# Linear attention and two feed-forward layers on one core: a new written-out order for phase one, the backward scan in its own buffer, no floor under the decays

## The chip, the cores and the metric

The kernel runs on 1 core of one Trainium2 chip. The metric is the device time of one execution in microseconds (us). Before the change three timed runs gave a median of 769.39 us (765.54 to 771.35).

## What is computed

```python
def _attn_ref(q, k, v, alpha):                      # B, H, S, D = 4, 8, 768, 48
    for t in range(S):
        state = alpha[:, :, t, :, None] * state + np.einsum('bhd,bhe->bhde', k[:, :, t], v[:, :, t])
        y[:, :, t] = np.einsum('bhd,bhde->bhe', q[:, :, t], state)

def _moe_ref(x, w_in, w_out, g_ln):                 # 3072 tokens, 384 -> 1024 -> 384
    h = x @ w_in
    e = np.exp(h - np.max(h, axis=-1, keepdims=True))
    solu = h * e / (np.sum(e, axis=-1, keepdims=True) + 1e-09)
    mu = np.mean(solu, axis=-1, keepdims=True)
    var = np.mean((solu - mu) ** 2, axis=-1, keepdims=True)
    return ((solu - mu) / np.sqrt(var + 1e-06) * g_ln) @ w_out

def _moe2_ref(x, w_in, w_out):                      # 384 -> 2048 -> 384
    h = x @ w_in
    return (h * np.cos(h)) @ w_out
```

The output of the attention, laid out as 3072 tokens of 384 features, goes through the first layer and then through the second. The weights arrive as 64-bit floats and are turned into 32-bit ones on the chip.

## The kernel before

The 3072 tokens are cut into 24 chunks of 128 tokens (6 chunks to each of 4 batches), numbered 0 to 23. Phase one takes each chunk through the attention and the first layer; phase two takes the second layer in 6 blocks of 512 tokens by 16 slices of 128 hidden units, 96 slots in all.

*Attention of a chunk.* A pack holds queries, keys and decays. `scan_to` (S1, line 256) multiplies the decays up along the chunk; `total_floor` (S2, line 263) writes the four totals, floored at 1e-30, into the start values `d1r` of the backward scan; `total_inverse` (S3, line 266) inverts them; `scan_from` (S4, line 270) scans backward and writes over the decays in the pack. The keys are multiplied by that result (KR on POOL, KV on DVE, line 277), the queries by the forward products (QP on POOL, QV on DVE, line 283). PE then makes the scores `pa` (SC), DVE masks them (MV), PE makes the values `px` (VA), turns the keys (TR) and makes the next state `pst` (ST); DVE adds the state (SD), POOL or ACT decays it (SP, SA).

*First layer of a chunk.* ACT and DVE split the values into a high and a low part (XH, XL), since every product is made of three matmuls in the 32-bit fast format. `hidden` (HD i.0 to i.2, line 392) makes 1024 hidden values in the single tile `ph`. Softmax and norm follow one after another: SM (DVE, maximum), EX (ACT, exponential with its sum), the guard (O1 on DVE, A1 on ACT, line 415), O2 (DVE), O3 (DVE, `so`, line 426), the mean (O4 on DVE, A4 on ACT), SQ (ACT), `variance` PA (ACT, line 444), PW (POOL), PB (ACT), NO (ACT). PE turns the result (TU), ACT and DVE split it (TH, TL), and two chunks together are projected (PR g.f, lines 483 to 490); PX (ACT, line 493) moves the projection to `x2T`. As `ph` and `so` have one buffer each, HD of a chunk waits for O3 of the chunk before.

*Weights.* A weight block is loaded (CL), shifted on DVE (C1, line 186), its sign and low part made on ACT (C2, CA), added on POOL (CD) or DVE (CV), split (WH on ACT, WL on POOL or WV on DVE), and, for the second layer, stored as 32-bit floats (WS). All loads are issued by the SyncE queue (SP), in the order of the list.

*Second layer.* `second_first` (SB, line 721) gives up the attention's memory. w2load (WD) loads a block, w2high (WA, ACT) and w2low (WG, POOL) split it; the loaded block has two buffers. XA (ACT) and XS (DVE) split `x2T`. A slot is h2 (PE), TN (ACT, turns), RS (DVE, residue), CS (ACT, sine of a shifted argument), CM (DVE), SH (ACT), SL (DVE) and three outputs (PE). Slots 0 to 2 are begun inside phase one; the rest come from the function `slot` (line 676), which the change leaves alone. Sine and exponential lie in different tables of ACT, and a load (ACT_TABLE_LOAD) stands where the next one needs the other table.

What sets the order is the written-out list `PLAN` (lines 67 to 118): words such as `S10` or `HD1.0` are called from the first to the last, and every engine gets its instructions in that order. Nothing is moved afterwards; an engine whose next instruction waits lets all those behind it wait.

Of the kernel before, what the change touches and what calls it, by code (L numbers as in the profile page):

```python
# [68 lines left out]
CL7 S21 S31 QP1 TR0 MV0 KT0 CV0 VA0 C21 C11 CA1 S41 ST0 WH0 XH0 LD3 C12 C22 XL0 WL0 CA2 SD0 C23 CV1 CA3 CV2 WH1 KV1
WH2 WV1 C24 TR1 CA4 SC1 S12 KT1 HD0.0 C13 C25 MV1 QP2 CA5 ST1 CV3 VA1 C14 WH3 C15 CV4 C26 CV5 LD4 XH1 WH4 S22 SD1 WL2  # L70
CA6 XL1 SA1 S32 WV3 S42 HD0.1 WH5 WV4 WV5 S13 HD0.2 QV3 S23 S33 KR2 SM0 S43 TR2 EX0 SC2 C16 A10 KT2 CV6 CL8 ST2 O20
KR3 WH6 O30 TR3 O40 C17 HD1.0 C27 MV2 WL6 CA7 SD2 HD1.1 KT3 CL9 CV7 SQ0 HD1.2 C18 SP2 PA0 WH7 ST3 SM1 PW0 VA2 S14 EX1
SC3 S24 LD5 S34 WL7 SD3 PB0 XH2 MV3 NO0 SP3 XL2 A11 TU0.0 C28 O21 TU0.1 C19 CA8 VA3 S44 TH0.0 CL10 O31 CD8 TH0.1 LD6
XH3 XL3 HD2.0 A41 SQ1 S15 HD2.1 C29 QV4 S25 PA1 KV4 WH8 HD2.2 TL0.0 PW1 QP5 TL0.1 SC4 SM2 PB1 NO1 WL8 TR4 MV4 EX2
TU1.0 TU1.1 S35 VA4 S45 KT4 A12 TH1.0 KV5 TH1.1 ST4 O22 O32 XH4 SC5 LD7 CA9 XL4 HD3.0 A42 CD9 SQ2 CL11 MV5 HD3.1 SD4
PA2 PW2 WH9 TL1.0 SP4 HD3.2 TL1.1 S16 PB2 VA5 C210 WV9 NO2 S26 PR0.0 S36 QP6 LD8 SM3 XH5 CA10 S46 EX3 XL5 KR6 TU2.0
A13 PX0.0 TU2.1 O23 TH2.0 PR0.1 O33 TH2.1 TL2.0 A43 SQ3 TL2.1 TR6 S17 PX0.1 SC6 KT6 S27 PA3 S37 QP7 ST6 MV6 PR0.2 PW3
SD6 PB3 NO3 S47 C110 TU3.0 PX0.2 C111 HD4.0 CL12 TH3.0 S18 HD4.1 S28 S38 KR7 TL3.0 HD4.2 QV8 S48 TR7 VA6 KT7 SM4 KR8
SC7 XH6 LD9 EX4 CD10 XL6 ST7 MV7 TR8 TU3.1 SD7 KT8 WS10 SC8 TH3.1 O14 O24 SP7 O34 C211 ST8 VA7 CA11 TL3.1 A44 CL13
CV11 SQ4 HD5.0 MV8 LD10 PA4 XH7 PW4 C212 XL7 HD5.1 WS11 C112 CA12 S19 PR1.0 PB4 CL14 NO4 CV12 QV9 C213 WS12 S29 S39  # L80
CA13 TU4.0 S49 HD5.2 PX1.0 TH4.0 SD8 KR9 VA8 SM5 SP8 TL4.0 EX5 SC9 LD11 C113 CV13 TR9 XH8 CL15 TU4.1 O15 C214 O25 WS13
MV9 PR1.1 CA14 C114 TH4.1 XL8 CD14 CL16 KT9 O35 ST9 PX1.1 VA9 S110 A45 WS14 SQ5 SD9 QP10 HD6.0 PA5 XH9 LD12 TL4.1 C215
PW5 XL9 HD6.1 CA15 SP9 PB5 NO5 S111 HD6.2 C115 TU5.0 S210 CL17 S211 TU5.1 S310 QP11 TH5.0 S311 PR1.2 SM6 TH5.1 CD15
TL5.0 EX6 TL5.1 PR2.0 O16 C216 WS15 O26 O36 PX1.2 CA16 S410 A46 SQ6 HD7.0 KV10 S411 PA6 PX2.0 TR10 SC10 C116 KT10 CV16
CL18 ST10 C117 C217 WS16 HD7.1 SD10 PW6 CA17 KR11 MV10 HD7.2 PB6 CL19 NO6 SP10 SC11 SM7 VA10 S112 EX7 QV12 TU6.0 XH10
LD13 O17 TU6.1 S212 TH6.0 S312 S412 PR2.1 TH6.1 TL6.0 KR12 TL6.1 XL10 PR2.2 PX2.1 O27 O37 C118 A47 SQ7 CV17 HD8.0 S113
WS17 PX2.2 PA7 C218 TR12 S213 S313 PW7 HD8.1 MV11 KT12 PB7 NO7 S413 HD8.2 CA18 C119 TU7.0 SM8 KR13 CL20 TU7.1 TH7.0
ST12 TH7.1 TL7.0 CD18 VA11 EX8 TL7.1 TR13 O18 C219 LD14 SD12 PR3.0 CA19 O28 O38 WS18 XH11 CL21 KT13 O48 QV13 SQ8 HD9.0
XL11 CV19 PX3.0 PA8 HD9.1 C220 WS19 PW8 S114 CA20 HD9.2 PB8 NO8 S214 C120 PR3.1 QV14 CL22 SM9 CD20 S314 EX9 C121 WS20
PR3.2 S414 PX3.1 C221 O19 KV14 CA21 O29 CV21 CL23 TR14 PX3.2 TU8.0 KT14 C122 WS21 TU8.1 TH8.0 ST13 O39 TH8.1 SC12 C222  # L90
TL8.0 HD10.0 A49 SQ9 TL8.1 MV12 HD10.1 PA9 CA22 PW9 SD13 PB9 CL24 HD10.2 NO9 C123 CV22 VA12 SM10 SP13 C223 WS22 SC13
CA23 LD15 XH12 CD23 TU9.0 MV13 EX10 CL25 TU9.1 ST14 XL12 TH9.0 SC14 WS23 C124 A110 C224 O210 O310 VA13 TH9.1 CA24
TL9.0 HD11.0 SD14 LD16 XH13 CD24 A410 SQ10 XL13 HD11.1 MV14 SP14 PA10 WS24 C225 TL9.1 HD11.2 PW10 CA25 S115 PB10 VA14
NO10 S215 SM11 QP15 TU10.0 XH14 LD17 S315 PR4.0 S116 EX11 XL14 QP16 TH10.0 TL10.0 PR4.1 S216 O111 PX4.0 C125 CV25 O211
WS25 S415 TU10.1 PX4.1 S316 KR15 PR4.2 O311 TH10.1 TL10.1 S416 HD12.0 PX4.2 O411 KR16 SQ11 HD12.1 PA11 PW11 HD12.2
PB11 NO11 TR15 SM12 TR16 KT15 TU11.0 KT16 TU11.1 SC15 TH11.0 TH11.1 TL11.0 ST15 EX12 TL11.1 ST16 SD15 PR5.0 O112 O212
SP15 O312 S117 A412 SQ12 PR5.1 S217 S317 QV17 PA12 PX5.0 S417 MV15 PW12 HD13.0 PX5.1 KR17 PB12 NO12 VA15 SC16 SD16
XH15 LD18 HD13.1 XL15 SP16 MV16 HD13.2 SC17 SM13 VA16 EX13 S118 TU12.0 A113 S218 XH16 LD19 O213 QP18 S318 TU12.1 MV17
TH12.0 PR5.2 TH12.1 O313 S418 HD14.0 PX5.2 O413 TL12.0 KR18 SQ13 HD14.1 TL12.1 S119 PA13 HD14.2 S219 S319 PW13 XL16
PB13 TR18 S419 NO13 VA17 QV19 KT18 SM14 KR19 ST18 XH17 LD20 SC18 XL17 EX14 SD18 TR19 A114 MV18 TU13.0 KT19 TU13.1  # L100
TH13.0 ST19 O214 O314 TH13.1 SC19 TL13.0 A414 VA18 SQ14 SD19 HD15.0 LD21 MV19 XH18 SA19 XL18 HD15.1 TL13.1 PA14 PW14
HD15.2 S120 PB14 NO14 S220 PR6.0 S320 QP20 SM15 S420 EX15 KV20 TU14.0 PX6.0 TU14.1 O115 TH14.0 O215 S121 TR20 TH14.1
# [5 lines left out]
XL22 HD18.1 HD18.2 VA23 SM18 EX18 TU17.0 TU17.1 PR7.1 TH17.0 O118 O218 O318 TH17.1 XH23 TL17.0 A418 SQ18 TL17.1 HD19.0
XL23 PA18 PX7.1 PW18 SB WD0 XA0 HD19.1 WD1 PB18 WD2 XS0 NO18 WD3 HD19.2 XA1 XA2 XS1 TU18.0 WA0 TU18.1 XS2 PR7.2 SM19
WG0 WA1 EX19 WG1 H20 A119 PX7.2 O219 O319 WA2 WA3 WG2 HD20.0 A419 TN0 SQ19 HD20.1 RS0 PA19 TH18.0 HD20.2 PW19 CS0  # L110
TL18.0 WG3 PB19 CM0 H21 TH18.1 SM20 NO19 TL18.1 EX20 PR8.0 A120 TN1 O220 SH0 RS1 TU19.0 PX8.0 TU19.1 TH19.0 SL0 PR8.1
TH19.1 O320 CS1 CM1 O420 SH1 TL19.0 HD21.0 SQ20 TL19.1 SL1 HD21.1 PA20 PX8.1 PW20 PB20 HD21.2 NO20 PR8.2 SM21 EX21
TU20.0 A121 PX8.2 O221 TU20.1 TH20.0 PR9.0 O321 TH20.1 TL20.0 O421 TL20.1 SQ21 HD22.0 PA21 PX9.0 PW21 HD22.1 PB21 NO21
HD22.2 TU21.0 SM22 TU21.1 TH21.0 PR9.1 TH21.1 TL21.0 EX22 TL21.1 O122 O222 O322 PR9.2 PX9.1 A422 SQ22 HD23.0 PA22
PX9.2 PW22 PB22 NO22 HD23.1 HD23.2 TU22.0 SM23 TU22.1 TH22.0 PR10.0 TH22.1 TL22.0 EX23 TL22.1 O123 O223 O323 PR10.1
PX10.0 A423 SQ23 PR10.2 PA23 PX10.1 PW23 PB23 NO23 TU23.0 PX10.2 TU23.1 TH23.0 H22 TH23.1 TL23.0 TL23.1 PR11.0 TN2 RS2
PR11.1 PX11.0 PR11.2 PX11.1 PX11.2
# [828 lines left out]
```

## Time and profile before

| | us |
|---|---|
| median of three timed runs | 769.39 |
| the profiled execution's own time | 772.82 |
| its span, first to last instruction | 771.0 |
| busy: PE / DVE / ACT / POOL | 734.4 / 598.5 / 443.9 / 148.6 |
| chain that ended last, share of PE / DVE / ACT | 67% / 9% / 6% |

PE's matmuls overlap in the profile, so its busy time shows where it stood idle, and not how fast it went; the granted clock (PEclk, 1.00 is 2.4 GHz and 0.50 is 1.2 GHz) is read beside it. An arrow in square brackets names what ended an engine's idle time before the instruction.

### The profile page before, as it was taken

Reading aid. Unit: us, or ns where it says so; the run is one execution under the profiler, and the core shown is the slowest. Engines: PE = TensorE matmul, PEld = TensorE weight load, DVE = VectorE, ACT = ScalarE, POOL = GpSimd, SP = SyncE. Lnnn points to the kernel's source line nnn. Section 1 sums busy time; section 2 is a strip of 40 time slices with the busy share of each in tenths; the row PEclk is TensorE's granted clock in tenths of the full one; section 3 lists DMA queues with packets and bytes.
Section 4 is the critical chain, followed back from the end, with each engine's and each line's share of the span. In section 5 each row is a group of like instructions: output and inputs, shape, how many; then the busy total and the mean of one; then the engine's idle time right before and its main releaser. Section 6 shows DMA issues by size and latency. Waiting matters only on the chain.

```text
span 771.0 us, 13377 instructions
## 1 busy us (share of the span) xinstructions
PE 734.4 (95%) x5260; PEld 612.5 (79%) x5260; DVE 598.5 (78%) x997; ACT 443.9 (58%) x748; POOL 148.6 (19%) x139
## 2 busy tenths in 40 slices
...
GB/s 237 260 134 153 114 231 256 163 282 264 34 87 87 88 43 62 21 1 1 84 88 102 62 102 103 34 144 76 82 62 110 82 83 140 85 101 92 14 1 45
DMA packets 27959, 81.15 MB, mean 105 GB/s; under 512 B 3600, under 2 KB 6928, under 8 KB 27888
## 3 DMA queue, kind: packets, MB, share of 16 engines
...
q14 instruction: 28, 0.23, 0.1%
...
## 4 chain that ended last, share of the span: by engine, by line
PE 67%; DVE 9%; ACT 6%; DMA 3%; issue 2%; POOL 1%; ACTq 0%; DVEq 0%; POOLq 0%
PE o L625 7%; PE ph L400 7%; PE o L623 7%; PE h L576 7%; PE o L624 7%; PE h L578 7%; PE h L577 7%; PE po L488 4%; PE po L489 3%; PE po L490 3%; PE px L333 2%; PE pl L467 2%; DVE wup L653 2%; PE pa L302 2%; DVE r L590 1%
## 5 line engine op out<-in xcount | busy, mean ns | idle before, releaser
L596 ACT ACTIVATE g<-r,halfpi 128x512 f32<-128x512 f32 x96 | 69.6, 725 | 117.8 <-DVE r L590 117.8
L625 PE MATMUL o<-gl,w2h 128*128 128x512 f32 x288 | 114.2, 397 | 2.3 <-DVE gl L611 2.3
L623 PE MATMUL o<-gh,w2h 128*128 128x512 f32 x288 | 113.4, 394 | 0.0
L576 PE MATMUL h<-x2h,w2h 128*128 128x512 f32 x288 | 113.4, 394 | 0.0
L577 PE MATMUL h<-x2l,w2h 128*128 128x512 f32 x288 | 113.2, 393 | 0.0
L624 PE MATMUL o<-gh,w2l 128*128 128x512 f32 x288 | 113.2, 393 | 0.0
L578 PE MATMUL h<-x2h,w2l 128*128 128x512 f32 x288 | 113.1, 393 | 0.0
L583 ACT ACTIVATE n<-h,quarter 128x512 int32<-128x512 f32 x96 | 65.9, 686 | 72.5 <-PE h L578 72.2
L589 DVE SCALAR_TENSOR_TENSOR r<-n,h 128x512 f32<-128x512 int32 x96 | 65.9, 686 | 48.8 <-ACT n L583 48.5
L601 DVE TENSOR_TENSOR g<-g,h 128x512 f32<-128x512 f32 x96 | 66.1, 688 | 34.2 <-ACT g L596 34.2
L488 PE MATMUL po<-lth,wout_h 128*128 128x256 f32 x288 | 83.3, 289 | 2.8 <-ACT x2T L494 2.8
L489 PE MATMUL po<-ltl,wout_h 128*128 128x256 f32 x288 | 81.5, 283 | 0.0
L490 PE MATMUL po<-lth,wout_l 128*128 128x256 f32 x288 | 81.4, 283 | 0.0
L590 DVE SCALAR_TENSOR_TENSOR r<-n,r 128x512 f32<-128x512 int32 x96 | 70.3, 732 | 3.3
L625 PEld LDWEIGHTS o<-gl,w2h 128*128 128x128 f32 x288 | 54.1, 188 | 17.4 <-DVE gl L611 5.1
L611 DVE TENSOR_TENSOR gl<-g,gh 128x512 fp32r<-128x512 f32 x96 | 66.1, 688 | 0.8 <-ACT gh L606 0.8
L624 PEld LDWEIGHTS o<-gh,w2l 128*128 128x128 f32 x288 | 54.2, 188 | 12.5
L577 PEld LDWEIGHTS h<-x2l,w2h 128*128 128x128 f32 x288 | 54.2, 188 | 12.4
L578 PEld LDWEIGHTS h<-x2h,w2l 128*128 128x128 f32 x288 | 54.1, 188 | 12.3
L576 PEld LDWEIGHTS h<-x2h,w2h 128*128 128x128 f32 x288 | 54.1, 188 | 12.3
L623 PEld LDWEIGHTS o<-gh,w2h 128*128 128x128 f32 x288 | 54.1, 188 | 11.9
L606 ACT ACTIVATE gh<-g 128x512 fp32r<-128x512 f32 x96 | 59.8, 623 | 2.8 <-DVE g L601 2.3
(117 smaller groups left out, 1432.6 us busy)
## 6 DMA issues: line engine op xcount, KB each, us to landing
...
wraw<-w SPq DMA_DIRECT2D x32, 384.0 KB, 3.1
...
w2f<-top SPq DMA_DIRECT2D x16, 384.0 KB, 5.8
w2r<-w2f SPq DMA_DIRECT2D x16, 384.0 KB, 2.9
...
```

The lines of the kernel that those rows point to most:

```text
L488: PE.matmul(po, wout_h[:, k, fs], lh[:, k, :], start=k == 0, stop=False)
L489: PE.matmul(po, wout_h[:, k, fs], ll[:, k, :], start=False, stop=False)
L490: PE.matmul(po, wout_l[:, k, fs], lh[:, k, :], start=False, stop=k == NF1 - 1)
L576: PE.matmul(ph, wh[:, ks], xh[:, k, :], start=k == 0, stop=False)
L577: PE.matmul(ph, wh[:, ks], xl[:, k, :], start=False, stop=False)
L578: PE.matmul(ph, wl[:, ks], xh[:, k, :], start=False, stop=k == KT - 1)
L590: V.scalar_tensor_tensor(out=r, in0=n, scalar=-C2, in1=r, op0=ALU.mult, op1=ALU.add)
L596: A.activation(g, r, AF.Sin, bias=halfpi)
L601: V.tensor_tensor(Gs[b, c], Gs[b, c], ph, ALU.mult)
L623: PE.matmul(po, wh[:, fs], gh, start=c == 0, stop=False)
L624: PE.matmul(po, wl[:, fs], gh, start=False, stop=False)
L625: PE.matmul(po, wh[:, fs], gl, start=False, stop=c == NF2 - 1)
```

## The change

The list is replaced by another (1123 words instead of 1147). In it no CS stands ahead of EX23, the last exponential; S2 is gone; the first loads, the last chunks of attention and the start of the second layer stand elsewhere. KV appears 13 times instead of 9 and KR 11 instead of 15, QP 14 instead of 12 and QV 10 instead of 12, CD 13 instead of 9 and CV 13 instead of 17, A1 17 instead of 11 and O1 7 instead of 13, SA 8 instead of 4 and SP 8 instead of 12. S4 writes into a buffer R of its own (two of them); d1r has one buffer instead of two; S3 reads the forward products directly; the padding rows of the first packs hold ones where they held zeros. A1 and PA are copies with a constant added, where they were Identity with a bias tile. The table of range checks (`out`) moves into a pool of phase two.

```diff
 PLAN = """
-LP0 LP1 MK LQ0 CL0 LQ1 LV0 ID S10 CL1 CL2 S20 CL3 S30 S40 CL4 CL5 LP2 KV0 LQ2 QV0 GL C20 LV1 C10 SC0 CA0 LV2 S11 CL6
...
+LP0 LP1 LP2 GL MK LQ0 LQ1 CL0 S10 CL1 CL2 S11 CL3 ID LV0 S30 S40 LQ2 LV1 LV2 QV0 KV0 QV1 SC0 S31 C20 C10 S41 CA0 C21
...
-        T["out"] = fl.tile([128, NCHK + NWB], F32, name="out")
...
-        tiny = cst.tile([128, 1], F32, name="tiny")
-        guards = cst.tile([128, 1], F32, name="guards")
...
-        d1r = [at.tile([128, AW], F32, name=f"d1r{j}", bufs=1) for j in range(2)]
+        d1r = at.tile([128, AW], F32, name="d1r", bufs=1)
...
-        def total_floor(i):
-            V.tensor_scalar(d1r[i % 2][:, C + 1::C + 1], T["P", i][:, :, C], 1e-30, None, ALU.max)
...
         def total_inverse(i):
-            total = d1r[i % 2][:, C + 1::C + 1]
-            V.reciprocal(total, total)
+            V.reciprocal(d1r[:, C + 1::C + 1], T["P", i][:, :, C])
...
         def scan_from(i):
...
-            V.tensor_tensor_scan(out=dec[:, back], data0=dec[:, back], data1=d1r[i % 2][:, back], initial=0.0,
+            R = at.tile([128, AW], F32, name=f"R{i}", tag="R", bufs=NR)
+            V.tensor_tensor_scan(out=R[:, back], data0=dec[:, back], data1=d1r[:, back], initial=0.0,
                                  op0=ALU.mult, op1=ALU.add)
+            T["R", i] = pairs(R[:, 1:])[:, :, 1:C + 1]
...
         def keys(i, eng=G):
...
-            K, R = pairs(pk[:, NP * C:2 * NP * C]), pairs(pk[:, 2 * NP * C + 1:])[:, :, 1:C + 1]
+            K, R = pairs(pk[:, NP * C:2 * NP * C]), T["R", i]
...
             else:
-                A.activation(c[:, 1:2], c[:, 1:2], AF.Identity, bias=guards)
+                A.activation(c[:, 1:2], c[:, 1:2], AF.Copy, bias=1e-9)
...
         def variance(i):
             c = T["c", i]
-            A.activation(c[:, 5:6], c[:, 4:5], AF.Identity, scale=1.0 / FF1, bias=tiny)
+            A.activation(c[:, 5:6], c[:, 4:5], AF.Copy, scale=1.0 / FF1, bias=1e-6)
...
-        for t in d1r + states:
+        for t in [d1r] + states:
...
-        G.memset(tiny, 1e-6)
-        G.memset(guards, 1e-9)
...
+            T["out"] = pools["q3"].tile([128, NCHK + NWB], F32, name="out", bufs=1)
...
-                   GL=lambda: SP.dma_start(gln, a["gln"]), S1=scan_to, S2=total_floor, S3=total_inverse, S4=scan_from,
+                   GL=lambda: SP.dma_start(gln, a["gln"]), S1=scan_to, S3=total_inverse, S4=scan_from,
...
+    pack0[..., 2 * NP * C:PW - 1] = np.arange(AW - 1) % (C + 1) > 0
```

DVE at the start of the program (P are the forward products, R the result of the backward scan, pk the packs, mage the first shifted weights), before:

```order
L259 SCALAR_TENSOR_TENSOR P_157<-pk_123,d1p 128x516
L264 TENSOR_SCALAR d1r_121<-P_157 128x4
L268 RECIPROCAL d1r_121<-d1r_121 128x4
L272 SCALAR_TENSOR_TENSOR pk_123<-pk_123,d1r_121 128x516
L280 TENSOR_TENSOR pk_123<-pk_123 128x512
L285 TENSOR_TENSOR pk_123<-pk_123,P_157 128x512
L186 TENSOR_SCALAR mage<-rawi_151 128x512
L259 SCALAR_TENSOR_TENSOR P_193<-pk_124,d1p 128x516
L264 TENSOR_SCALAR d1r_122<-P_193 128x4
L268 RECIPROCAL d1r_122<-d1r_122 128x4
```

and in the changed kernel (line numbers are its own, 4 or 5 less):

```order
L256 SCALAR_TENSOR_TENSOR P_149<-pk_119,d1p 128x516
L256 SCALAR_TENSOR_TENSOR P_155<-pk_120,d1p 128x516
L262 RECIPROCAL d1r<-P_149 128x4
L267 SCALAR_TENSOR_TENSOR R_163<-pk_119,d1r 128x516
L281 TENSOR_TENSOR pk_119<-pk_119,P_149 128x512
L276 TENSOR_TENSOR pk_119<-pk_119,R_163 128x512
L281 TENSOR_TENSOR pk_120<-pk_120,P_155 128x512
L262 RECIPROCAL d1r<-P_155 128x4
L183 TENSOR_SCALAR mage<-rawi_147 128x512
L267 SCALAR_TENSOR_TENSOR R_185<-pk_120,d1r 128x516
```

Two forward scans now come first, S2 is no longer there, the product of the queries stands ahead of that of the keys, and the second chunk's queries follow at once.

The SyncE queue at the start, which issues the loads (rawi are blocks of the first weights, pk packs, v values), before:

```order
L240 DMA pk_123<-pack 128x1024
L180 DMA rawi_151<-win 128x1024
L240 DMA pk_124<-pack 128x1024
L247 DMA v_154<-vpack 128x448
L727 DMA ident<-ident 128x128
L180 DMA rawi_159<-win 128x1024
L180 DMA rawi_161<-win 128x1024
L180 DMA rawi_164<-win 128x1024
L180 DMA rawi_168<-win 128x1024
L180 DMA rawi_170<-win 128x1024
```

and in the changed kernel (line numbers are its own, 4 or 5 less):

```order
L237 DMA pk_120<-pack 128x1024
L177 DMA rawi_147<-win 128x1024
L177 DMA rawi_151<-win 128x1024
L177 DMA rawi_153<-win 128x1024
L177 DMA rawi_157<-win 128x1024
L722 DMA ident<-ident 128x128
L244 DMA v_160<-vpack 128x448
L237 DMA pk_121<-pack 128x1024
L244 DMA v_166<-vpack 128x448
L244 DMA v_168<-vpack 128x448
L177 DMA rawi_194<-win 128x1024
L177 DMA rawi_218<-win 128x1024
```

The third pack's decays are loaded third of all (above these rows); its queries and keys and two more blocks of values now stand ahead of the fifth and sixth weight blocks.

ACT where the last chunks of phase one meet the first slots (e is the exponential, g the sine, w2h the high part of a weight block of the second layer, x2h that of its input, n the turns), before:

```order
L438 ACTIVATE c_3636<-c_3636 128x1
L583 ACTIVATE n_0_3669<-h_0_0_3643,quarter 128x512
L442 ACTIVATE e_3640,c_3636<-so_3656,c_3636 128x1024
L446 ACTIVATE c_3636<-c_3636,tiny 128x1
L475 ACTIVATE lth_3682<-pl_0_3599 128x4x128
L596 ACT_TABLE_LOAD
L596 ACTIVATE g_0_3692<-r_0_3678,halfpi 128x512
L454 ACTIVATE c_3636<-c_3636 128x1
L475 ACTIVATE lth_3682<-pl_1_3605 128x4x128
L459 ACTIVATE so_3656<-so_3656,c_3636 128x1024
L412 ACT_TABLE_LOAD
L412 ACTIVATE e_3713,c_3709<-ph_3661,c_3709 128x1024
```

and in the changed kernel (line numbers are its own, 4 or 5 less):

```order
L548 ACTIVATE w2h_3813<-w2r_3811 128x768
L548 ACTIVATE w2h_3817<-w2r_3815 128x768
L548 ACTIVATE w2h_3824<-w2r_3822 128x768
L490 ACTIVATE x2T<-po_1_3897 128x256
L434 ACTIVATE c_3876<-c_3876 128x1
L438 ACTIVATE e_3881,c_3876<-so_3922,c_3876 128x1024
L442 ACTIVATE c_3876<-c_3876 128x1
L559 ACTIVATE x2h_3834<-x2T 128x512
L450 ACTIVATE c_3876<-c_3876 128x1
L408 ACTIVATE e_3987,c_3982<-ph_3931,c_3982 128x1024
L455 ACTIVATE so_3922<-so_3922,c_3876 128x1024
L490 ACTIVATE x2T<-po_2_3957 128x256
```

Before, the sine of slot 0 stands ahead of an exponential with a table load on either side; now three blocks of w2 are split in a row, then a chunk's square, the last part of x2h and the last exponential follow, and no table load is among them.

## Rows read from the trace of the kernel before

**Rows 1.** Windows: from:to, length, PE, PEld, DVE, ACT, POOL busy, PEclk, DMA share, GB/s.

```profile
0.00:20.00 20.00, 11.62 (x78) 6.37 (x78) 15.20 (x24) 9.49 (x15) 5.07 (x15) 0.91 0.66 230
20.00:40.00 20.00, 14.55 (x128) 10.70 (x130) 17.32 (x24) 8.98 (x17) 4.48 (x3) 0.76 0.85 249
40.00:60.00 20.00, 13.70 (x196) 10.82 (x192) 18.40 (x25) 15.22 (x27) 10.06 (x7) 0.91 0.61 166
...
180.00:200.00 20.00, 17.75 (x224) 16.05 (x223) 16.04 (x28) 11.88 (x23) 7.37 (x7) 1.00 0.77 209
...
300.00:320.00 20.00, 17.16 (x91) 15.28 (x90) 10.93 (x19) 17.09 (x28) 4.22 (x3) 0.83 0.22 70
```

**Rows 2.** Timeline of PE, 40 to 62 us: start us, us, engine, line, op, tiles [idle before <-releaser].

```profile
44.15 1.19 PE L400 MATMUL ph<-win_h,xh 128*128 128x512 f32 x2 [1.53 <-DVE so L429]
...
60.76 1.22 PE L400 MATMUL ph<-win_h,xh 128*128 128x512 f32 x2 [2.66 <-DVE so L429]
```

**Rows 3.** Groups by line of DVE, only 0 to 60.2 us.

```profile
L264 DVE TENSOR_SCALAR d1r<-P 128x4 f32<-128x4 f32 x5 | 1.9, 370 | 0.2
```

**Rows 4.** Timeline of DVE, 0 to 30 us.

```profile
4.97 0.17 DVE L264 TENSOR_SCALAR d1r<-P 128x4 f32<-128x4 f32 x1
...
7.99 0.69 DVE L280 TENSOR_TENSOR pk<-pk 128x512 f32<-128x512 f32 x1 [1.37 <-DMA pk<-pack]
...
10.87 1.18 DVE L264 TENSOR_SCALAR d1r<-P 128x4 f32<-128x4 f32 x1
...
23.12 1.23 DVE L259 TENSOR_TENSOR_SCAN P<-pk,d1p 128x516 f32<-128x516 f32 x1 [2.54 <-DMA pk<-pack]
```

**Rows 5.** Timeline of POOL, 0 to 30 us.

```profile
10.84 1.18 POOL L285 TENSOR_TENSOR pk<-pk,P 128x512 f32<-128x512 f32 x1 [8.23 <-DVE P L259]
```

**Rows 6.** Groups by line, whole run: count | busy us, mean ns | idle before us.

```profile
L557 POOL TENSOR_TENSOR w2l<-w2r,w2h 128x768 fp32r<-128x768 f32 x16 | 29.6, 1853 | 37.1 <-ACT w2h L553 37.1
...
L367 DVE TENSOR_TENSOR S<-pst,S 64x256 f32<-64x256 f32 x32 | 13.3, 417 | 2.0 <-PE px L333 1.5 <-PE pst L351 0.2
...
L442 ACT ACTIVATE e<-so,c 128x1024 f32<-128x1024 f32 x24 | 27.6, 1151 | 3.9 <-DVE c L436 2.1 <-DVE d1r L264 1.1
...
L564 ACT ACTIVATE x2h<-x2T 128x512 fp32r<-128x512 f32 x18 | 11.0, 616 | 0.0
...
L186 DVE TENSOR_SCALAR top<-raw 128x768 int32<-128x768 int32 x16 | 11.0, 691 | 1.0 <-DMA w2f<-top 1.0
...
L446 ACT ACTIVATE c<-c,tiny 128x1 f32<-128x1 f32 x24 | 7.0, 292 | 0.6
...
L264 DVE TENSOR_SCALAR d1r<-P 128x4 f32<-128x4 f32 x24 | 6.9, 292 | 0.6
...
L438 ACT ACTIVATE c<-c 128x1 f32<-128x1 f32 x15 | 3.0, 201 | 8.6 <-DVE so L429 8.6
...
L412 ACT ACT_TABLE_LOAD x2 | 2.6, 1283 | 0.0
```

**Rows 7.** Timeline of ACT, 296 to 324 us.

```profile
305.69 0.58 ACT L475 ACTIVATE lth<-pl 128x512 fp32r<-128x512 f32 x1
...
306.29 1.28 ACT L596 ACT_TABLE_LOAD   x1
```

**Rows 8.** Timeline of PE, 305 to 321 us.

```profile
307.77 0.28 PE L490 MATMUL po<-lth,wout_l 128*128 128x256 f32 x1
...
310.22 0.28 PE L490 MATMUL po<-lth,wout_l 128*128 128x256 f32 x1
...
314.37 0.58 PE L488 MATMUL po<-lth,wout_h 128*128 128x256 f32 x1 [2.84 <-ACT x2T L494]
...
314.96 0.41 PE L490 MATMUL po<-lth,wout_l 128*128 128x256 f32 x1
...
319.44 0.41 PE L490 MATMUL po<-lth,wout_l 128*128 128x256 f32 x1
```

**Rows 9.** DMA issues by line: count, KB each, median us to landing.

```profile
w2r<-w2f SPq DMA_DIRECT2D x16, 384.0 KB, 2.9
```

More of the change, by code (lines that the diff above doesn't have):

```diff
@@ L39 @@
 NPK = 3
+NR = 2
 LA = 4
@@ L67 @@
 PLAN = """
-LP0 LP1 MK LQ0 CL0 LQ1 LV0 ID S10 CL1 CL2 S20 CL3 S30 S40 CL4 CL5 LP2 KV0 LQ2 QV0 GL C20 LV1 C10 SC0 CA0 LV2 S11 CL6
[L69 to L102, printed above, removed]
```

63 lines of the change are left out of this document (48 added, 15 removed).

## The prediction

> **What bounds the kernel now.** I read the windows first, by stage [rows 1]. In the first 60 us PE is busy for 11.6, 14.6 and 13.7 of 20 us each, while DVE is busy for 15.2, 17.3 and 18.4: DVE leads there. From 80 us on PE shows idle time only here and there (2.25 us in 180 to 200), and in 300 to 320, where the first slots of phase two meet the last exponentials: 2.84 us idle and a granted clock of 0.83. So the rest of the kernel is PE's own work, which the change leaves as it is, and what can be won or lost lies at those two places.
>
> Then I asked what ends PE's waits in the start. Both times that PE waits for the hidden matmuls of the next chunk (44.15 and 60.76 us) it is DVE's `so` (L429, word O3) that lets it go [rows 2]. DVE's queue up to O30 and O31 therefore sets when chunks 1 and 2 begin.
>
> **The start.** Up to O31 the old and the new list give DVE almost the same work. Out go five S2, which took 1.9 us together [rows 3]; behind O31 move one shift, C19 (0.69 by its group's mean), and the two instructions of SD3 (2 x 0.42) [rows 6]. Two key and query products leave this stretch and two others enter it, with the same shape and cost. Sum: 1.9 + 0.7 + 0.8 = 3.4 us less.
>
> DVE also waits less for loads, or for others. Before, the forward scan at 23.12 us waited 2.54 us for the third pack [rows 4]; LP2 now stands third of all loads, so this wait goes. The 1.37 us wait for the queries and keys [rows 4] stays in its place, though 0.26 MB more lies ahead of them, since a second forward scan of 1.23 us stands in the gap. What is late next is the fifth weight block: LQ2, LV1 and LV2 (0.52 + 2 x 0.23 = 0.98 MB by their shapes in the order) now stand in front of it, and at the 230 to 249 GB/s of these windows [rows 1] that is up to 4.1 us; it is nothing if the block's buffer comes free later than that anyway. What queues behind its shift C14 on DVE is XL0, and for that PE waits with the first hidden matmuls. I take 1.0 us, nearer to nothing, because DVE has its scans, masks and adds of four blocks in front of C14. Start: 3.4 + 2.5 - 1.0 = 4.9 us earlier.
>
> At one place a rule bears on this. The S2 at 4.97 us took 0.17 us; the one at 10.87 took 1.18, and began and ended with POOL's product at 10.84 [rows 4, 5]: DVE stood still while POOL ran. The Trainium skill (SBUF — State Buffer, Who interferes with whom) says that the two share a port pair, that whoever comes first holds it for its whole instruction, and that this holds for two-port modes of DVE and for DVE instructions with two SBUF inputs. By that rule the new list can lose as well as win, since CD puts four more adds on POOL: it is the slower rival below, where its price comes from rows.
>
> **The stretch from 60 to 300 us.** The other 19 S2 cost 6.9 - 1.9 = 5.0 us of DVE [rows 3, 6], beside a PE that has work. Its idle time here that rows name is the 2.25 us [rows 1]; the rest is nothing or small. Bounds 0 and 2.3 us, or a loss of as much where the new order waits elsewhere; I take 1.0 us. The copies in place of Identity (PA 24 times, A1) save 0.29 - 0.20 = 0.09 us each [rows 6], on ACT, and A1 takes six guards from DVE: nothing, since PE's other chunk covers the chain, and at most some tenths where it doesn't. Writing R instead of the pack costs DVE nothing (same shape, 1.2 us); two buffers make S4 of chunk i wait for the keys of chunk i - 2, long done. d1r with one buffer is written and read by DVE alone, in order. Four more SA fall on ACT, which is idle for two fifths of the span; if ACT were bound they would cost 4 x 4 x 0.3, some 5 us, at the 0.29 us of PA's row [rows 6].
>
> **The junction.** Before, ACT loads the sine's table at 306.29 us and the exponential's again after it, 1.28 us each [rows 6, 7], twice over ahead of the last exponential. PE waits 2.84 us for an `x2T` copy that is behind them at ACT, and then goes at half clock: three projection matmuls take (319.44 - 314.96) / 7 = 0.64 us instead of (310.22 - 307.77) / 7 = 0.35 [rows 8], over eight such triplets 2.3 us. Together 5.1 us. Of five loads (three of the sine, two of the exponential) one is left, and it stands after the last exponential, beside three projections.
>
> What is late next: ACT now splits the w2 blocks 1, 2 and 3 in a row. Block 3 needs block 1 split by POOL (1.85) and its load (2.9) [rows 6, 9], so 4.75 us after WA1, and ACT has only WA2 in between. Queued behind are PX, A4, SQ22 (1.15 and its accumulator read), PA and XA2 (0.62) [rows 6], then XS2 on DVE, and H20 on PE waits for it: some 4.75 + 0.85 + 2.75 + 0.7 = 9.05 us after WA1, which ends some 0.5 us after PE begins HD23. PE has HD23 and PR9.2 before H20: 18 matmuls of 512 columns and 24 of 256 at the full pace [rows 8], 4.2 + 2.8 = 7.0 us. So PE waits about 2.5 us. Bounds: 0, if the earlier blocks leave ACT free sooner, and 4.75 with another spell at half clock. Junction: 5.1 - 2.5 = 2.6 us.
>
> A rule would make this larger. The load at 306.29 starts as the copy before it ends (305.69 + 0.58) [rows 7], so each costs ACT its 1.28 us and no more. The Trainium skill (ScalarE: Activation LUTs, What ACT_TABLE_LOAD costs) gives 2.66 us to each switch, with a drain of 1.38; by that the four loads that go would be worth up to 5.5 us more. The trace does not agree.
>
> **Sum.** 4.9 + 1.0 + 2.6 = 8.5 us. The profiled execution took 772.8 us (span 771.0 and 1.8 around it), so 764.3; it lies 3.4 above the median of the timed runs, and against that median, 769.4, I predict 760.9 us. One per cent, 7.7 us, is about what a measurement of this kernel can tell from no change.
>
> **Rivals.**
> - *The start gains nothing*: the fifth block comes the full 4.1 us late, or DVE's shorter queue ends in another wait. For it: PE's waits in the start end with DVE after loads [rows 2, 4]. Against it: five S2 are gone in any case. Gain 3.6, so 765.8 us.
> - *POOL blocks DVE (slower)*. POOL is busy for 5.1 + 4.5 + 10.1 = 19.6 us of the first 60 [rows 1]. If about half of that already holds DVE up, as S2 at 10.87 suggests for its share, a list that lets all of it do so loses 10 us more: -8.5 + 10 gives 770.9 us. It decides from 8.5 us of added blocking on. Against it: KR's four moves take work from POOL.
> - *The clock falls at the junction again*: the 2.5 us wait and 2.3 us at half clock, as before. Gain 6.2, so 763.2 us.
> - *More is won*: no wait at the junction and no late block: 4.9 + 1.0 + 1.0 + 5.1 = 12.0, so 757.4 us.
>
> **How the numbers follow.** Forecast 0.50 (its own range 756 to 766), start gains nothing 0.20, POOL blocks 0.10, clock 0.12, more 0.08. Faster by over 1% means under 761.7: a little over half of the forecast, all of the last rival, and a part of the clock's (0.28 + 0.08 + 0.09): 0.45. Slower by over 1% needs POOL's rival and lost time later too: 0.07. Within 1%: 0.48. The range, 753 to 771, reaches from below the last rival to the slower one.
>
> **What would show it.** In the changed kernel's trace: hidden matmuls of chunk 2 begin near 56 us instead of 60.8; no S2; one sine load, and none of the exponential's after the first; a PE wait of 2 to 3 us ahead of slot 0's first matmul, and PEclk near 1.00 there. The prediction is wrong if chunk 2 begins no earlier, if DVE's two-input instructions stretch beside POOL more than now, or if PE finds new waits between 60 and 300 us.

## The result, and the profile after

| | before | after |
|---|---|---|
| median us | 768.89 (4 runs, 765.54 to 771.35) | 756.35 (4 runs, 755.58 to 756.80) |
| ratio, 95% interval | | 0.9839 (0.9813 to 0.9866) |
| profiled execution, its span | 772.82, 771.0 | 756.13, 754.2 |
| busy PE / DVE / ACT / POOL | 734.4 / 598.5 / 443.9 / 148.6 | 730.0 / 582.7 / 438.8 / 154.4 |

The gain is 12.5 us between the medians, where 8.5 was forecast; the two profiled executions lie 16.7 apart, because that of before was a long one. Besides being shorter, the runs after lie within 1.2 us of each other, those of before within 5.8.

The same windows as [rows 1], of the changed kernel (length, then busy us of PE, PEld, DVE, ACT, POOL, then PEclk, DMA share and GB/s):

```profile
0.00:20.00 20.00, 13.00 (x82) 7.79 (x82) 14.07 (x21) 9.52 (x16) 6.72 (x13) 0.83 0.92 338
20.00:40.00 20.00, 15.11 (x200) 11.02 (x201) 19.05 (x31) 14.40 (x27) 7.36 (x5) 0.83 0.75 186
40.00:60.00 20.00, 18.50 (x240) 15.16 (x240) 18.63 (x28) 19.09 (x36) 11.40 (x9) 1.00 0.71 189
180.00:200.00 20.00, 20.00 (x273) 17.98 (x272) 15.05 (x25) 10.80 (x22) 4.61 (x4) 1.00 0.29 61
300.00:320.00 20.00, 20.00 (x179) 18.05 (x178) 9.69 (x16) 12.46 (x24) 6.42 (x4) 1.00 0.16 46
```

PE has 4.8 us more work in 40 to 60 us, no idle time in the two later windows, and full clock in 300 to 320 us, where it had 0.83. In 60 to 300 us its idle time falls from 4.1 to 1.9 us.

PE's timeline where [rows 2] showed it waiting for chunks 1 and 2 (start us, us, operation, idle time before):

```profile
39.62 0.70 PE L396 MATMUL ph<-win_h,xh 128*128 128x512 f32 x2 [1.46 <-DVE so L425]
...
50.37 0.73 PE L396 MATMUL ph<-win_h,xh 128*128 128x512 f32 x2
```

Chunk 1's hidden matmuls start 4.5 us earlier, and chunk 2's 10.4 us earlier and without a wait.

DVE's timeline in the start, the places that answer to [rows 4] and the two instructions that were longest for their kind:

```profile
3.58 2.36 DVE L256 TENSOR_TENSOR_SCAN P<-pk,d1p 128x516 f32<-128x516 f32 x2 [2.05 <-DMA pk<-pack]
...
9.44 0.69 DVE L281 TENSOR_TENSOR pk<-pk,P 128x512 f32<-128x512 f32 x1 [0.77 <-DMA pk<-pack]
...
16.51 1.41 DVE L198 CUSTOM_DVE_ANT_0 magso<-magso,rawi 128x1024 uint16<-128x1024 uint16 x1 [0.28 <-ACT rawi L194]
...
25.19 1.23 DVE L256 TENSOR_TENSOR_SCAN P<-pk,d1p 128x516 f32<-128x516 f32 x1
...
26.78 0.17 DVE L262 RECIPROCAL d1r<-P 128x4 f32<-128x4 f32 x1
...
35.98 2.11 DVE L267 TENSOR_TENSOR_SCAN R<-pk,d1r 128x516 f32<-128x516 f32 x1
...
48.36 1.28 DVE L425 SCALAR_TENSOR_TENSOR so<-e,c,ph 128x1024 f32<-128x1024 f32 x1
```

Two forward scans in a row start at 3.58; the queries and keys cost a wait of 0.77 where it was 1.37; the scan of the third pack, which had waited 2.54, waits for nothing at 25.19. `so` of chunk 1 starts at 48.36 where it started at 59.45.

So the start won 11.1 us on DVE, and the forecast accounts for less than half of it. The rest shows in the trace of before once DVE and POOL are read side by side. DVE before, instructions that took longer than others of their line:

```profile
15.38 1.43 DVE L186 TENSOR_SCALAR mage<-rawi 128x512 int32<-128x512 int32 x1
...
26.44 1.41 DVE L186 TENSOR_SCALAR mage<-rawi 128x512 int32<-128x512 int32 x1
...
34.22 1.67 DVE L221 TENSOR_TENSOR win_l<-magso,win_h 128x512 fp32r<-128x512 f32 x1
...
51.12 2.20 DVE L259 TENSOR_TENSOR_SCAN P<-pk,d1p 128x516 f32<-128x516 f32 x1
...
56.67 2.86 DVE L272 TENSOR_TENSOR_SCAN pk<-pk,d1r 128x516 f32<-128x516 f32 x1
```

and POOL before, in the same stretch:

```profile
14.73 1.81 POOL L221 TENSOR_TENSOR win_l<-mage,win_h 128x512 fp32r<-128x512 f32 x1 [2.70 <-ACT win_h L215]
26.05 1.51 POOL L285 TENSOR_TENSOR pk<-pk,P 128x512 f32<-128x512 f32 x1 [9.52 <-DVE am L318]
...
33.80 1.54 POOL L280 TENSOR_TENSOR pk<-pk 128x512 f32<-128x512 f32 x1 [4.80 <-DVE pk L272]
...
50.40 1.83 POOL L221 TENSOR_TENSOR wout_l<-topo,wout_h 128x768 fp32r<-128x768 f32 x1 [1.27 <-ACT wout_h L215]
...
56.33 2.10 POOL L201 TENSOR_TENSOR topo<-topo,lowo 128x768 int32<-128x768 int32 x1 [0.91 <-ACT lowo L197]
```

Each of the five starts while a POOL instruction runs, and ends 0.3 to 1.1 us after it: the shift at 15.38 lies beside POOL's 14.73 to 16.54 and takes 1.43 in place of 0.42. Three more (27.77, 40.79 and 47.46 us) and S2 at 10.87 [rows 4, 5] did the same. Against what the same instructions take elsewhere (0.17, 0.42, 0.55, 0.67, 0.95, 1.23), the nine lose 9.2 us. In the changed kernel only the add at 16.51 (1.41 for 0.69) and the scan at 35.98 (2.11 for 1.23) do: 1.6 us. POOL isn't less busy there (25.5 us in the first 60, where it was 19.6): it runs beside other DVE instructions. From the first scan to that `so` DVE is busy for 40.2 of 44.8 us, where it was 49.8 of 55.8: its waits fell by 1.4 us only, and of the 9.6 us less of busy time 7.6 are POOL's and some 2.0 are work.

The junction in the changed kernel, ACT's timeline at its last split of a w2 block, the last part of `x2h` and the first sine:

```profile
319.45 0.85 ACT L548 ACTIVATE w2h<-w2r 128x768 fp32r<-128x768 f32 x1 [4.03 <-DMA w2r<-w2f]
...
322.07 0.62 ACT L559 ACTIVATE x2h<-x2T 128x512 fp32r<-128x512 f32 x1
...
327.27 1.28 ACT L591 ACT_TABLE_LOAD   x1
```

PE's timeline there, at chunk 23's first hidden matmul, slot 0's first and the turns behind it:

```profile
315.92 0.63 PE L396 MATMUL ph<-win_h,xh 128*128 128x512 f32 x2
...
322.92 0.39 PE L571 MATMUL h<-x2h,w2h 128*128 128x512 f32 x1
...
325.47 1.09 PE L463 MATMUL pl<-ident,so 128*128 128x128 f32 x8 [0.33 <-ACT so L455]
```

ACT waits 4.03 us for w2 block 3, much as forecast, and PE doesn't wait: slot 0 starts at 322.92, right behind its predecessor, and the next wait, for the norm, is 0.33. Only one table load for the sine is left (327.27), and behind it none for the exponential.

### The profile page after: what moved, and what is told of

Its sections match the earlier page's. It is cut to its first block, busy times and chain, and to the rows that moved or that the text cites. A ratio compares the mean times of both kernels' runs of the same rounds, so it can differ in the third digit from the quotient of the medians.

```text
span 754.2 us, 13336 instructions
## 1 busy us (share of the span) xinstructions
PE 730.0 (97%) x5260; PEld 606.5 (80%) x5260; DVE 582.7 (77%) x965; ACT 438.8 (58%) x766; POOL 154.4 (20%) x134
## 4 chain that ended last, share of the span: by engine, by line
PE 44%; DVE 8%; ACT 3%; issue 1%; ACTq 0%
PE o L620 7%; PE h L571 7%; PE h L573 7%; PE h L572 7%; PE o L618 7%; PE o L619 7%; DVE wup L648 2%; DVE r L584 2%; DVE r L585 2%; ACT g L591 1%; DVE g L596 1%; DVE wup L649 1%; PE po L484 1%; PE po L485 1%; PE po L486 1%
## 5 line engine op out<-in xcount | busy, mean ns | idle before, releaser
L618 PEld LDWEIGHTS o<-gh,w2h 128*128 128x128 f32 x288 | 54.1, 188 | 12.6 <-ACT x2T L490 0.2
```

Source lines behind the costliest of these rows:

```text
L618: PE.matmul(po, wh[:, fs], gh, start=c == 0, stop=False)
```

## The experiments

Two theories. **W** (work and loads, the record's own): the start is won by less DVE work and by the third pack's load. **P** (POOL): the new list puts POOL's work beside DVE instructions that it doesn't hold up. For the end of phase one, **J**: the order of sine and exponential is what cost there. Medians, each with its ratio to runs of the kernel before on the same chip. Differences below are between the medians; "by the ratios" means that each version is first set against before on its own chip:

| run | us (runs) | ratio, 95% interval |
|---|---|---|
| changed kernel | 756.35 (4) | 0.9839 (0.9813 to 0.9866) |
| old_order | 765.44 (10) | 0.9968 (0.9948 to 0.9988) |
| new_start | 763.43 (10) | 0.9938 (0.9914 to 0.9963) |
| new_late | 767.82 (10) | 0.9997 (0.9975 to 1.002) |
| new_to_3 | 760.43 (6) | 0.9899 (0.9865 to 0.9934) |
| old_to_14 | 764.18 (10) | 0.9944 (0.9916 to 0.9972) |
| pool_small | 763.31 (10) | 0.9932 (0.9903 to 0.9961) |
| pool_busy | 763.66 (10) | 0.9938 (0.9918 to 0.9958) |
| late_pack | 755.46 (4) | 0.9833 (0.9792 to 0.9875) |
| floor_back | 758.85 (6) | 0.9883 (0.9859 to 0.9907) |
| sine_early | 760.61 (6) | 0.9913 (0.9888 to 0.9938) |
| keep_warm | 755.93 (6) | 0.9852 (0.9827 to 0.9877) |
| both | 756.05 (6) | 0.983 (0.9793 to 0.9866) |

### Which stretch carries the gain

Five kernels have the changed code and a list put together from the two. In the first three, chunk 10's backward scan starts from chunk 11's totals (the old list has S3 of 11 ahead of S4 of 10, and `d1r` has one buffer now).

**old_order** (against the changed kernel, as all diffs here but one)

```diff
 PLAN = """
-LP0 LP1 LP2 GL MK LQ0 LQ1 CL0 S10 CL1 CL2 S11 ...
+LP0 LP1 MK LQ0 CL0 LQ1 LV0 ID S10 CL1 CL2 CL3 ...
```

> The changed code with the old list, its 24 S2 words struck out. Theory W (work and loads: the start is won by less DVE work and the earlier third pack, the junction by the table loads): only the floors go, 1.9 us in the start and about 1 later, so hidden matmuls of chunk 2 near 59 us (60.8 before) and about 766 us. Theory P (POOL: the new list is faster at the start because DVE stands still beside POOL for some 1.6 us there and not for 9): the list carries the gain, and the 1.0 us that S2 stood still at 10.87 us passes to the next DVE instruction, so chunk 2 at 59.5 us or later and 767 to 769 us.

2.5 us faster than before by the ratio (1 to 4). The time is W's (P had 767 to 769), and chunk 2's hidden matmuls come at 56.4 us, earlier than either theory had it. In DVE's timeline, the mask at the place where S2 had stood still, and the scan of the third pack:

```profile
10.93 1.21 DVE L314 TENSOR_TENSOR am<-pa,mask 128x1024 f32<-128x1024 f32 x1
...
21.31 1.23 DVE L256 TENSOR_TENSOR_SCAN P<-pk,d1p 128x516 f32<-128x516 f32 x1 [2.49 <-DMA pk<-pack]
```

The 1.0 us of S2 didn't pass on, as P had it: the reciprocal and the mask that stand there now take 0.18 and 1.21. Up to `so` of chunk 1 DVE stands still beside POOL for 5.0 us, in six instructions, where it was 9.2 in nine: part of that went with the code alone. The wait for the third pack stays. The code carries about a fifth of the gain, the order the rest.

**new_start** and **new_late**: up to HD4.0 the new list, then the old; and up to HD18.0 the old, then the new.

> The changed code; the new list up to HD4.0, from there the old one without S2. Both theories W and P: the start's gain is kept, hidden matmuls of chunk 4 near 80 us (91.2 before) and 758 to 761 us, with the two sine loads and PE's 2.8 us wait near slot 0 still there. Rival K (the time won at the start is only lent, and the old order waits for it later): chunk 4 near 80 us but over 765 us.

> The changed code; the old list without S2 up to HD18.0, then the new one. Junction theory J (the sine's and the exponential's table loads and the half clock behind PE's wait cost about 5 us): one sine load, no wait of PE over 1 us and a granted clock of 1.00 between chunk 20 and slot 2, and 763 to 765 us. Rival: the junction is gained only because phase one arrives there with DVE and ACT ahead, by the start: under 2 us less than the old list with the new code.

Neither came in at its forecast time: new_start is 2.0 us under old_order, new_late 2.4 over it, and both for the way they were cut. In new_start chunk 4 begins at 79.3 us, as expected; then PE waits, since the words that the old list has for it there were done in the new prefix. In new_late HD19 to HD21 stand without the scores, values and projections that the whole new list puts between them. PE in new_start:

```profile
83.29 0.66 PE L463 MATMUL pl<-ident,so 128*128 128x128 f32 x4 [2.31 <-ACT so L455]
```

and in new_late, one of three such waits:

```profile
285.54 0.73 PE L396 MATMUL ph<-win_h,xh 128*128 128x512 f32 x2 [1.38 <-DVE so L425]
```

A list may only be cut where both have done the same words, so the cuts were made again there.

**new_to_3**: new up to LD7 (the load of chunk 7's pack and values), just ahead of chunk 3 (four words differ), then old. **old_to_14**: old up to NO13 (one word differs), then new.

> The changed code; the new list up to LD7, just before chunk 3's hidden matmuls, where both lists have done the same words but four; from there the old list (S3 of chunk 11 one word later). Theory P or W, the start's gain is the start's own: chunk 3 at 60.5 to 61 us as in the changed kernel (66.9 with the old list and the new code), kept through chunk 5 this time, and 759 to 761.5 us against 765.4 of the old list with the new code. Rival K (lent only): chunk 3 at 61 but chunk 12 again near 191 us, as with the old list, and 763 us or more.

> The changed code; the old list up to NO13, where both lists have done the same words but one, then the new list, with one table load for the sine. Theory J (table loads and the half clock behind the wait): no wait of PE over 0.6 us between 280 and 340 us, granted clock 1.00 there, 4 to 5 us less than the old list with the new code: 760.5 to 761.5 us. Rival (the junction is gained only with a start that is ahead): 763.5 us or more, with waits of PE for `so` between chunks 18 and 22.

new_to_3 gains 0.69% more than old_order by the ratios, 5.3 us: the start. Chunk 3 begins at 59.1 us, 7.8 us ahead of old_order, and 3.6 of these are gone by chunk 12 (187.4 against 191.6 us), so rival K holds in part. PE's timeline in new_to_3:

```profile
176.47 0.65 PE L463 MATMUL pl<-ident,so 128*128 128x128 f32 x4 [1.97 <-ACT so L455]
```

and ACT's:

```profile
173.01 1.10 ACT L190 ACTIVATE low<-raw 128x768 bf16<-128x768 f32 x1 [2.10 <-DMA raw<-w]
```

ACT waits for the load of a w2 block, then PE for ACT: the old list has its weights too late for a program that is ahead. This wait, and some 1.6 us at the lower clock behind it (0.57 granted in 177 to 181 us), are most of the 3.6. The changed kernel has no wait of PE in 165 to 190 us; its list stands one to two weight blocks further at chunk 8.

old_to_14 has PE idle for 0.38 us in 300 to 340 us, at full clock, and without a wait between chunks 18 and 22, as J has it, but its time is the rival's: 0.24%, 1.8 us under old_order by the ratios (1.3 in the medians, 3.6 in the profiled executions, 762.43 and 766.04). The runs of both spread over 4 to 5 us. The traces say more: from the norm of chunk 13 (NO13) to slot 0's first output old_to_14 takes 130.6 us and old_order 134.0, so the new end is worth 3.3 us there, in one execution of each.

### POOL beside DVE

**pool_small** (the kernel before; the low parts are set to zero beforehand)

```diff
-            eng.tensor_tensor(lo, w, hi.bitcast(F32), ALU.subtract)
+            m = 32 if eng is G and n in (0, 2, 6, 7) else w.shape[1]
+            eng.tensor_tensor(lo[:, :m], w[:, :m], hi.bitcast(F32)[:, :m], ALU.subtract)
...
-            eng.tensor_tensor(K, K, R, ALU.mult)
+            w = 8 if eng is G and i in (2, 3) else C
+            eng.tensor_tensor(K[:, :, :w], K[:, :, :w], R[:, :, :w], ALU.mult)
...
-            eng.tensor_tensor(Q, Q, P[:, :, 1:C + 1], ALU.mult)
+            w = 8 if eng is G and i in (1, 2) else C
+            eng.tensor_tensor(Q[:, :, :w], Q[:, :, :w], P[:, :, 1:w + 1], ALU.mult)
```

> The kernel before, with eight POOL instructions of the first 55 us (two products of queries, two of keys, four low parts of weights) cut to a sixteenth or so of their columns; that part of the computation is left out, the queries of chunks 1 and 2 are zeros and the sine's argument is scaled by 0.999. DVE's list is untouched. Theory P: the DVE instructions that took 1.2 to 2.2 us beside POOL (S2 at 10.87, shifts at 15.38, 26.44 and 27.77, a low part at 34.22, an add at 40.79, a scan at 51.12) take their 0.2 to 1.2 us, chunk 2's hidden matmuls come 5 to 7 us earlier (54 to 56 us) and the whole takes 762 to 765 us. Theory W: DVE does the same work, chunk 2 stays within 1 us of 60.8 and the time within 1.5 us of before.

The same instructions on DVE, in the order of before, with little beside them on POOL:

```profile
10.60 0.25 DVE L265 TENSOR_SCALAR d1r<-P 128x4 f32<-128x4 f32 x1
...
14.18 0.40 DVE L186 TENSOR_SCALAR mage<-rawi 128x512 int32<-128x512 int32 x1
...
30.89 0.69 DVE L222 TENSOR_TENSOR win_l<-magso,win_h 128x512 fp32r<-128x512 f32 x1
...
46.92 1.22 DVE L260 TENSOR_TENSOR_SCAN P<-pk,d1p 128x516 f32<-128x516 f32 x1
...
51.49 1.23 DVE L273 TENSOR_TENSOR_SCAN pk<-pk,d1r 128x516 f32<-128x516 f32 x1
```

0.25 for 1.18, 0.40 for 1.43, 0.69 for 1.67, 1.22 for 2.20, 1.23 for 2.86; one shift, beside a product on POOL that was left whole, still takes 1.20. Chunk 2 at 53.95 us in place of 60.76; 5.2 us faster in the medians, with DVE's list untouched. W is out as the whole of it.

**pool_busy** (the changed kernel)

```diff
+        scratch = x2T[:, 2, NTOK - 512:]
+        G.memset(scratch, 0.0)
...
+                   GX=lambda i: [G.tensor_tensor(scratch, scratch, scratch, ALU.add) for _ in range(i)],
```

with GX8 (eight such sums) behind MK, GX5 behind WL2, GX2 behind QP2, GX1 behind KR2 and GX2 behind KR3.

> The changed kernel with 18 more POOL instructions (128x512 sums on memory that nobody reads until the end of phase one), put where POOL is idle in the first 42 us: 8 before its first product, 5 behind the second low part, 2, 1 and 2 later. DVE's list is untouched. Theory P: DVE instructions with operands in SBUF stand still beside them; DVE's busy time in the first 40 us grows by 5 us or more, chunk 2 comes at 53 to 58 us instead of 50.4, and the time is 759 to 764 us. Theory W: POOL's time beside DVE costs nothing; chunk 2 within 0.7 us of 50.4, 756 to 757 us.

DVE's timeline in it:

```profile
8.69 1.46 DVE L281 TENSOR_TENSOR pk<-pk,P 128x512 f32<-128x512 f32 x1
...
12.96 0.17 DVE L262 RECIPROCAL d1r<-P 128x4 f32<-128x4 f32 x1
...
14.14 2.06 DVE L267 TENSOR_TENSOR_SCAN R<-pk,d1r 128x516 f32<-128x516 f32 x1
...
16.71 1.21 DVE L314 TENSOR_TENSOR am<-pa,mask 128x1024 f32<-128x1024 f32 x1
```

and POOL's, the first eight and the next five added sums:

```profile
2.61 12.51 POOL L734 TENSOR_TENSOR x2T<-x2T 128x512 f32<-128x512 f32 x8
...
23.16 5.97 POOL L734 TENSOR_TENSOR x2T<-x2T 128x512 f32<-128x512 f32 x5
```

A product of 0.69 takes 1.46, a scan of 1.23 takes 2.06; the reciprocal (0.17) and the mask on scores in PSUM (1.21) take what they always do. Chunk 2 comes at 57.99 us, 7.6 later, and the kernel is 7.3 us slower. DVE stands still for 12.6 us up to `so` of chunk 1 (1.6 in the changed kernel); its waits, 1.4 us in place of 4.6, take up a part of that. One sign of P's failed: DVE's busy time in the first 40 us grew by 3.1 us and not by 5, as it got through 42 instructions there in place of 51. That POOL holds DVE up, and that the kernel pays for it, is shown from both sides: taken away in the old order, put back in the new.

### The terms one by one

**late_pack**: `LP2` (the load of the third pack's decays) behind `CL5` in the changed list.

> The changed kernel with the third pack's decays loaded at their old place, behind the sixth weight block. Theory W: DVE's third forward scan waits about 2.5 us again, `so` of chunks 0 and 1 come 2 to 2.5 us later and the time is 758.4 to 759 us. Theory P: in the new list that scan stands at 25.2 us, when the pack is there in either place; no wait, and 756 to 757 us.

The scan of the third pack, in late_pack:

```profile
23.70 1.23 DVE L256 TENSOR_TENSOR_SCAN P<-pk,d1p 128x516 f32<-128x516 f32 x1
```

No wait, and no loss: W's 2.54 us isn't won by the load. This scan (S12) is DVE's 30th instruction from the first scan on in the new list and was the 23rd in the old; by then the pack is there from either place.

**floor_back**

```diff
-            V.reciprocal(d1r[:, C + 1::C + 1], T["P", i][:, :, C])
+            total = d1r[:, C + 1::C + 1]
+            V.tensor_scalar(total, T["P", i][:, :, C], 1e-30, None, ALU.max)
+            V.reciprocal(total, total)
```

> The changed kernel with the floor under the totals back (24 instructions of 128x4 on DVE, each right ahead of its reciprocal). The record's step: 1.9 us of DVE in the start and up to 1.0 later, so 758.3 to 759.3 us. Rival P: a floor alone costs 0.2 us of DVE; five in the start 1.0, and the 0.37 us mean of before was POOL's doing: 756.8 to 757.8 us. If neither shows, under 756.8, DVE has that much slack at its waits for loads and for PE.

2.5 us slower than the changed kernel, 1.0 of it by chunk 2 (51.4 us). The whole time is the one of the record's step, the start is P's. The five floors of the start, as a group by line:

```profile
L263 DVE TENSOR_SCALAR d1r<-P 128x4 f32<-128x4 f32 x5 | 1.8, 366 | 0.1
```

and two of them in DVE's timeline:

```profile
5.80 0.14 DVE L263 TENSOR_SCALAR d1r<-P 128x4 f32<-128x4 f32 x1
...
26.66 1.18 DVE L263 TENSOR_SCALAR d1r<-P 128x4 f32<-128x4 f32 x1
```

The mean is that of [rows 3] again: four take 0.14 to 0.17, and one stands still beside POOL (26.37 to 27.81 us there). In the changed kernel the reciprocal at 26.78 lies beside POOL's product at 26.50 and takes 0.17. The floor was of a kind that POOL holds up, its neighbour isn't.

**sine_early**: EX23, O123, O223 and O323 behind CS0.

> The changed kernel with the last exponential and the three DVE words of chunk 23 behind it (EX23, O123, O223, O323) moved behind the first sine (CS0), so that ACT loads the exponential's table and the sine's once more. Theory J (at the junction the order sine before exponential is what costs): the turns of chunk 23 come 3 us later or more, PE waits 2 to 3 us ahead of them and goes at half clock behind that; 758.5 to 760.5 us. Rival: two loads of 1.28 us lie beside PE's work and cost nothing: within 0.7 us of 756.4.

ACT's timeline there:

```profile
329.62 1.28 ACT L408 ACT_TABLE_LOAD   x1
330.92 1.11 ACT L408 ACTIVATE e<-ph,c 128x1024 f32<-128x1024 f32 x1
...
334.06 0.37 ACT L490 ACTIVATE x2T<-po 128x256 f32<-128x256 f32 x1
```

and PE's one wait:

```profile
334.48 0.38 PE L484 MATMUL po<-lth,wout_h 128*128 128x256 f32 x1 [2.80 <-ACT x2T L490]
```

4.3 us slower. PE waits 2.80 us for an `x2T` copy (ACT 334.06) behind the exponential, nearly the 2.84 of [rows 8], but its granted clock stays at 1.00 in this run; of the 3.5 us between the profiled executions 2.9 arise here. J holds: the order alone makes that wait.

### Two attempts at more

**keep_warm**

```diff
+        def keep_warm(n):
+            w = ps.tile([128, 512], F32, name=f"warm{len(T)}", tag="rot", bufs=3)
+            for j in range(n):
+                PE.matmul(w, d1p[:, 0:128], d1p[:, 0:512], start=True, stop=True)
```

with six behind SC0, two each behind HD0.1 and HD0.2.

> The changed kernel with ten more matmuls of the kind that warms TensorE at the start (0.63 us each), six behind the first scores, two ahead of and two behind the last third of chunk 0's hidden matmuls, where PE is idle for 4.2, 1.9 and 1.4 us. If the half clock at 12.0 to 18.8 and 29.1 to 35.9 us holds DVE up (it waits 1.20 and 0.73 us for products that take 1.9 to 2.1 us there and 1.1 at full clock): granted clock 1.00 in both stretches, chunk 1's hidden matmuls 1.5 to 2.5 us before 39.6, 754 to 755 us. Rival: DVE's own work sets the start, chunk 1 within 0.5 us, 755.9 to 756.9 us.

Its first window (columns as above):

```profile
0.00:20.00 20.00, 17.90 (x111) 9.49 (x112) 14.61 (x23) 10.55 (x17) 6.11 (x13) 1.00 0.92 336
```

and two instructions of DVE's timeline:

```profile
26.76 0.56 DVE L183 TENSOR_SCALAR topo<-rawo 128x768 int32<-128x768 int32 x1 [1.37 <-DMA rawo<-wout]
...
35.61 1.22 DVE L314 TENSOR_TENSOR am<-pa,mask 128x1024 f32<-128x1024 f32 x1 [1.04 <-PE pa L298]
```

The clock is 1.00 up to 20 us and chunk 0's hidden matmuls come 1.0 us earlier. Then DVE waits 1.37 for the next weights and 1.04 for scores that the added matmuls had delayed, and chunk 1 is 0.5 us late. Nothing is left in the time. The second stretch was tried only in part: in 30 to 40 us the granted clock went from 0.70 to 0.83.

**both**: LP2 behind CL5, three such matmuls behind SC0 and three ahead of HD0.2.

> An attempt at a better kernel: the changed one with the third pack loaded behind the sixth weight block, three matmuls of the warming kind behind the first scores and three right ahead of the last third of chunk 0's hidden matmuls, both where PE is idle for 3 us with the pack late. If the half clock near 12 to 19 us costs DVE its waits for products there (1.3 us): granted clock near 1.00 from 0 to 20 us, chunk 0's hidden matmuls at 18 us or earlier, 754 to 755 us. Rival: what is won by 20 us is waited for again at the loads of the next weights (DVE waited 0.7 us for one at 25.6 with the pack late, 1.37 with the warming matmuls): 755 to 756 us, no better than the late pack alone at 755.5.

DVE's timeline in it:

```profile
26.57 0.56 DVE L183 TENSOR_SCALAR topo<-rawo 128x768 int32<-128x768 int32 x1 [2.08 <-DMA rawo<-wout]
```

The rival: the clock is 1.00 up to 20 us, but chunk 0's hidden matmuls come at 19.5 us and not by 18, and the wait for the weights grows to 2.08 us. Of the versions tried, late_pack, keep_warm, both and the changed kernel can't be told apart.

## Why the prediction was right or wrong

*Direction and size.* Faster by 1.6%, and inside the range; the size was a third too small, and the chances put "faster by over 1%" (0.45) below "within 1%" (0.48). "More is won" (757.4 us, chance 0.08) describes the outcome best. Its two conditions came true: no late block, no wait at the junction.

*The start, 4.9 us.* In the trace chunk 2 is 10.4 us ahead, twice the forecast (50.4 us, where 56 was foreseen): 4.3 with the code alone (old_order) and 6.0 with the list. In the time new_to_3 shows 5.3 by the ratios, with 3.6 lost on the way, plus about 1 for the floors. That this is near 4.9 is luck, for two of the three terms were wrong. **Less DVE work**, 3.4: the floors' 1.9 were 0.9 of work and 1.0 of standing beside POOL, as floor_back shows again; the rest (C19, SD3) moved as stated, but C19 took 0.54 and not its group's mean of 0.69. **The third pack**, 2.5: the wait went, but late_pack shows that the load's place has nothing to do with it; the scan's place has. Other waits came (1.20 and 0.73 us for PE), so that all of DVE's waits fell by 1.4. **The fifth block**, -1.0: it never was late; its shift (C14) went at 20.87 us without a wait. What stands in their place is POOL: 9.2 us of DVE standing still fell to 5.0 with the code alone and to 1.6 with the list. The prediction saw the mechanism and its first case (S2 at 10.87). Its rival even took about half of POOL's 19.6 us as holding DVE up already, near the 9.2 measured, and yet it could only lose. The failing step is this term of the sum, put at nothing: before's other long durations were taken as those of the instructions, though their group's mean was of two kinds, 0.42 and 1.43. The Trainium skill (SBUF — State Buffer, Who interferes with whom) has the rule that sorts them: a DVE instruction with at most one input in SBUF and outside the two-port modes doesn't contend. The reciprocal (0.17 beside POOL) and the masks agree; the floor and the shifts, held up, are of the form (tensor_scalar) that it says can enter those modes.

*The middle, 1.0.* PE's idle time in 60 to 300 us was 4.1 us and not only the 2.25 of the row, and it fell by 2.2. floor_back puts 1.7 us (HD20 at 287.3 against 284.6, less the 1.0 of the start) on the other 19 floors alone, and new_to_3 shows a wait for weights that the new list avoids. Mis-sized by half, in the direction of the upper bound.

*The junction, 2.6.* The loss before was read rightly: sine_early brings 2.80 of the 2.84 back, without the half clock, and old_order has both (a wait of 2.75 us, 0.68 granted in 305 to 315 us). The 2.5 us put against it didn't come. ACT's wait for the load was there (4.03), and from WA1's end (314.7 us) to the end of XS2 (323.4) it took 8.7 us where 9.05 were reckoned; but WA1 ended 1.2 us before HD23 began, not 0.5 after. And "H20 on PE waits for it" was wrong: slot 0's second matmul, at 323.15, reads `x2l` while XS2 still runs, since the first six need only its first two thirds. The traces of old_order and old_to_14 put the end at 3.3 us.

*The sum.* By the ratios the parts are 2.5 (code), 5.3 (start) and 1.8 (end): 9.6 of 12.5, each with an interval of 1.5 us or more to either side. The traces narrow it: slot 0's first output begins at 357.2 us in old_order, 353.2 in new_to_3 and 348.3 in the changed kernel. Of these 9.0 us (9.1 between the medians) 4.0 are what is left of the start, and 5.0 come from the rest of the list, 3.3 of them at the end by old_to_14. The other 1.7 lie in chunks 3 to 13 or in what the parts do together; no run separates them.
